# The last four output tiles in another order: tile three behind the first half of tile four, and both halves of tile four in PSUM banks of the gate pool

## The chip, the cores and the metric

The kernel runs on one core of one Trainium2 chip. The metric is device time in microseconds (us) of one execution. The kernel before takes 214.47 us, the median of three runs (214.2 to 214.63).

A core has five engines with an instruction stream each, which wait for one another through counting semaphores: TensorE (PE in the profile; its weight loads are PEld), VectorE (DVE), ScalarE (ACT), GpSimd (POOL) and SyncE (SP), which here mainly issues DMAs. A name with a q (PEq, SPq) is the engine's sequencer: waits, branches and DMA issues.

## The reference, cut to what matters

The inputs are one sequence of 2048 rows of 448 numbers, in bf16. Both branches read the same normalised rows, and their results are added to the input.

```python
def _A_ref(x, wqkv, wo):          # 16 heads of 28, causal window of 256 rows
    q, k, v = heads(x @ wqkv)
    scores = where(0 <= i - j < 256, q @ k.T * 28 ** -0.5, -1e9)
    return (softmax(scores) @ v) @ wo

def _B_ref(x, w_gate, w_up, w_down):   # 448 -> 1792 -> 448
    return (gelu(x @ w_gate) * (x @ w_up)) @ w_down

xn = layernorm(A_x)
out = A_x + _A_ref(xn, A_wqkv, A_wo) + _B_ref(xn, B_w_gate, B_w_up, B_w_down)
```

## The kernel before, in words

The 2048 rows are handled in four query blocks of 512 (`qb` 0 to 3), each of four tiles of 128 rows. A block goes through attention (scores, softmax weights, the product with v, scaling into `oN`), then through the feed-forward part (`gated`: seven pairs of gate and up matmuls, GELU on ScalarE, the product on VectorE into `hT`), and last through `gen_down`, which makes the output rows. The whole order is written out by hand: each engine works its instructions in the order in which the Python code emits them. For blocks 0 to 2 the steps of `gen_down` are spread between the next block's attention steps. For block 3 nothing follows, so `gen_down(3)` stands at the end of the program alone. The change touches only that end.

One output tile is a sum of 18 matmuls into one PSUM bank: 14 with `hT` and `wd` (contraction over 1792), and 4 with `oN` and `wo`. `gen_down` names three lists of them: `main`, ten `hT` chunks that are ready early; `late`, the four chunks of the last two gate pairs; `os`, the four `oN` chunks. `part` issues one such list for a tile, `whole` opens a tile and issues all 18. `begin` takes a bank, and `end` does the rest: VectorE adds the input rows (`res`, L382), the bank is given back, SyncE stores the result (L384). `res` has two buffers that are used in turn, so an addition waits until the store that read its buffer two results ago has landed. The second half of tile four (`lo` above 0) has a buffer of its own, of tag `wa`.

The rows of the last block's tiles are called one to four here (`tt` 0 to 3, rows 1536 to 2047), the column halves of tile four 4a and 4b (224 columns each). Before the change the order is: `main` of one and two; `late` of one and two; `main` and `late` of three; `os` of one, two and three; then all 18 of 4a and all 18 of 4b. In tiles two and three each matmul is issued as two of 224 columns (`ws`, L390), in tile one as one of 448.

PSUM has eight banks. Four (`b0` to `b3`) are handed out by `take` and returned by `give`, with `held` as the list of those in use. The other four are two buffers of two banks each, of tag `s` in the pool `phase[0].pool`; the gates use them in turn (`gt`), ScalarE's GELU reads them, and after the last gate they are free.

The tile framework derives the waits between engines from the tiles that instructions read and write: a matmul that writes to a tile waits, where needed, for the instructions that read the tile before.

Two things lie between the steps. VectorE computes a flag from the softmax sums (L874 to L883), and after 48 steps of `gen_down(3)` every engine loads it (L887); at the very end each engine branches on it around a general path, which does not run here. After the last addition POOL copies the last result twice (L890, L891), and VectorE writes one column (L892).

Of the kernel before, what the change touches and what calls it, by code (L numbers as in the profile page):

```python
# [13 lines left out]
f32 = mybir.dt.float32  # L14
i32 = mybir.dt.int32

S, D, H, Dh, F = 2048, 448, 16, 28, 1792
P = 128
NT = S // P
NF = F // P  # L20
QB, NB = 512, 4
# [6 lines left out]
def kernel(  # L28
# [11 lines left out]
    nc = tc.nc  # L40
# [8 lines left out]
    phase = [None]  # L49
# [152 lines left out]
    held = {}  # L202

    def take(name, cols=QB, tag=None):

        tag = tag or spare[0]
        spare.remove(tag)  # L210
        ps = psum.tile([P, QB], f32, name=name, tag=tag, bufs=1)[:, 0:cols]
        held[id(ps)] = tag, ps
        return ps

    def give(*tiles):
        for ps in tiles:
            spare.append(held.pop(id(ps))[0])
# [94 lines left out]
    def gen_pairs(qb, order):  # L312

        def v_pair(t):
            two = [take("pv", D) for _ in range(2)]
            for c in range(7):
                for hi, ps in enumerate(two):
                    r = slice(64 * hi, 64 * hi + 64)
                    w = wv[r, 3, :] if c == 6 else wv[r, c // 2, :] if c % 2 == hi else wvs[r, c // 2, :]
                    nc.tensor.matmul(ps, lhsT=xchunk(qb, hi, c, (t + hi) * P, P), rhs=w, start=c == 0, stop=c == 6,  # L320
                                     tile_position=(64 * hi, 0), skip_group_check=True)
                if c < 6:
                    yield
            for i in range(2):
                v_copy(t + i, two[i], nc.vector.tensor_copy if i or not t % 4 or qb == 1 else nc.scalar.copy)
            yield

        def qk_pair(g):
            two = [take("p" + part) for part in "qk"]
            for c in range(7):  # L330
                for hi, ps in enumerate(two):
                    r, hs = slice(64 * hi, 64 * hi + 64), slice(4 * g, 4 * g + 4)
                    w = w3p[r, hs, :] if c == 6 else (wqp, wkp)[hi][r, c // 2, hs, :] if c % 2 == hi else wsq[r, c // 2, hs, :]
                    nc.tensor.matmul(ps, lhsT=w.rearrange("p h d -> p (h d)"), rhs=xchunk(qb, hi, c, qb * QB, QB), start=c == 0,  # L334
                                     stop=c == 6, tile_position=(64 * hi, 0), skip_group_check=True)
                if c < 6:
                    yield
            qk_copies(qb, g, *two, nc.vector.tensor_copy if (g != 1) == (qb == 1) else nc.scalar.copy)
            yield

        return chain(*(v_pair(4 * qb + n) if kind == "v" else qk_pair(n) for kind, n in order))
# [25 lines left out]
    def gen_down(qb):  # L367

        hT, oN = hTs[qb], oNs[qb]
        fs = [(hT, wd, f) for f in range(NF)]  # L370
        main, late, os = fs[0:5] + fs[7:12], [fs[f] for f in (5, 12, 6, 13)], [(oN, wo, g) for g in range(4)]

        def begin(tt, lo=0, up=D):
            return tt, take("po", up - lo), lo, up

        def end(tt, po, lo, up):
            t, w = 4 * qb + tt, up - lo
            if lo:
                res = work.tile([P, 2 * QB], bf16, name="res", tag="wa", bufs=1)
            else:  # L380
                res = work.tile([P, D], bf16, name="res", bufs=2)
            nc.vector.tensor_tensor(out=res[:, 0:w], in0=po[:, 0:w], in1=x_sb[:, t, lo:up], op=ALU.add)  # L382
            give(po)
            nc.sync.dma_start(out=outv[:, t, lo:up], in_=res[:, 0:w])  # L384
            last_res[:] = [res]

        def part(o, terms, start=False, stop=False):
            tt, po, lo, up = o
            w = up - lo
            ws = (0, w // 2, w) if 4 * qb + tt in (NT - 3, NT - 2) else (0, w)  # L390
            for n, (x, wt, k) in enumerate(terms):
                for a, b in zip(ws, ws[1:]):
                    nc.tensor.matmul(po[:, a:b], lhsT=x[:, k, tt * P:(tt + 1) * P], rhs=wt[:, k, lo + a:lo + b],  # L393
                                     start=start and n == a == 0, stop=stop and n == len(terms) - 1, skip_group_check=True)
                if stop and n == len(terms) - 1:
                    end(*o)
                yield

        def whole(terms, *o):
            yield from part(begin(*o), terms, True, True)  # L400

        if qb < NB - 1:
            two = [begin(tt) for tt in range(2)]
            for o in two:
                yield from part(o, main + late, True)
            for o in two:
                yield from part(o, os[0:3])
            for tt, po, *_ in two:
                r = slice(64 * tt, 64 * tt + 64)
                nc.tensor.matmul(po, lhsT=oN[r, 3, tt * P:(tt + 1) * P], rhs=wo[r, 3, :], start=False, stop=True,  # L410
                                 tile_position=(64 * tt, 0), skip_group_check=True)
            for o in two:
                end(*o)
            yield
            for tt in (2, 3):
                yield from whole(main + late + os, tt)
        else:
            three = [begin(tt) for tt in range(3)]
            for terms, start in ((main, True), (late, False)):
                for o in three[0:2]:  # L420
                    yield from part(o, terms, start)
            yield from part(three[2], main + late, True)
            for o in three:
                yield from part(o, os, False, True)
            for lo, up in ((0, D // 2), (D // 2, D)):
                yield from whole(main + late + os, 3, lo, up)

    def new_hT(qb):
        hT = blk.tile([P, NF, QB], bf16, name="hT", tag="hT")
# [369 lines left out]
    for qb in range(NB):  # L799
# [4 lines left out]
        if qb == 0:  # L804
# [3 lines left out]
            w = gen_pairs(1, (("v", 0), ("v", 2), ("k", 0), ("k", 1), ("k", 2)))  # L808
# [4 lines left out]
                    [lambda: stat(11), (w, 7), lambda: rstd(8, 4), "sums", "inverse", (w, 7)]]  # L813
        else:
            d = gen_down(qb - 1)
            if qb < 3:
                u = gen_pairs(qb + 1, (("v", 0), ("k", 0), ("v", 2), ("k", 1), ("k", 2)))
# [64 lines left out]
    nc.vector.tensor_reduce(out=ok1, in_=okr, axis=AX.X, op=ALU.min)  # L882
    nc.vector.tensor_copy(out=flag[:, :], in_=ok1)  # L883
    last = gen_down(NB - 1)
    for _ in range(48):
        next(last)
# [136 lines left out]
```

## Time and profile before

| what | value |
|---|---|
| time, median of three runs | 214.47 us (214.2 to 214.63) |
| span of the profiled execution, first to last instruction | 213.1 us |
| PE busy | 207.6 us, 97% of the span |
| DVE, ACT, POOL busy | 74%, 62%, 23% |
| share of PE in the chain that ended last | 94% |
| last block's output matmuls on PE (L393) | 195.24 to 209.2 us |
| last addition on VectorE | 209.21 to 209.60 us |

No separate device time is listed for the profiled execution; the median time stands 1.4 us above its span, which is what lies outside the first and the last instruction.

How to read the profile: times in rows of the timeline are microseconds from the span's start, then the length of the merged row; a matmul's length contains its run through the array, so matmuls that follow each other overlap in the rows, and their spacing is what counts. In brackets stands how long the engine sat idle before a row, and what ended the wait. In the waits view a row reads: who waited, for whom, total time, how often, the longest.

### The profile page before, as it was taken

The numbers are of one execution on the slowest core, as the hardware profiler recorded it, in microseconds if no ns is written. First come the engines' busy times: TensorE is split into PE (matmuls) and PEld (weight loads), VectorE is DVE, ScalarE is ACT, GpSimd is POOL, SyncE is SP. The second block draws the span as 40 slices with busy tenths as digits, with TensorE's granted clock in tenths as the row PEclk, the third lists the DMA queues.
The fourth block names the chain that finished last, engine by engine and source line by source line (L and its number), as shares of the span: only waits on it lengthen the run. The fifth ranks groups of instructions, "written<-read, shape, count | busy, mean of one in ns | idle before, by whom it ended". The sixth has DMA issues, their size and how long they took to land.

```text
span 213.1 us, 6428 instructions
## 1 busy us (share of the span) xinstructions
PE 207.6 (97%) x2722; PEld 101.2 (47%) x2722; DVE 157.5 (74%) x355; ACT 131.6 (62%) x123; POOL 48.6 (23%) x86
## 2 busy tenths in 40 slices
PE   7999999999999999999999999999999999999992
PEld 2433444444454545444445445444445444544992
DVE  7899998999767985796536997495483898479531
ACT  4699578566777977423777887532676877665000
POOL 5287658451000220041000201022000022006001
PEclk9999999999999999999999999999999999999998
DMA  6999969979420101003421000001000101000011
GB/s 184 280 221 215 106 172 220 243 241 171 110 53 25 37 20 26 8 5 65 74 74 46 25 0 29 20 0 30 16 3 0 47 4 45 6 0 0 26 45 49
DMA packets 23993, 15.67 MB, mean 74 GB/s; under 512 B 9208, under 2 KB 23832, under 8 KB 23960
## 3 DMA queue, kind: packets, MB, share of 16 engines
q1 hardware_dynamic: 22918, 14.87, 31.2%
q8 instruction: 22, 0.36, 0.7%
q10 hardware_dynamic: 1042, 0.34, 0.7%
q14 instruction: 11, 0.09, 0.1%
HBM read 9.26 MB, written 2.41 MB: 55 GB/s over the span
## 4 chain that ended last, share of the span: by engine, by line
PE 94%; DVE 1%; ACT 1%; DMA 1%; issue 1%; DVEq 0%; ACTq 0%
PE po L393 26%; PE gt L456 20%; PE u L456 12%; PE ue L456 8%; PE pq L334 7%; PE sc L652 6%; PE ov L624 5%; PE pv L320 4%; PE pq L191 2%; PE pv L191 1%; DMA x_sb<-in_A_x_dram 1%; ACT p_sb L656 1%; DVE st L155 1%; PE s L191 1%; PE pk L191 1%
## 5 line engine op out<-in xcount | busy, mean ns | idle before, releaser
L656 ACT ACTIVATE p_sb<-sc 128x2048 bf16<-128x2048 f32 x39 | 73.2, 1878 | 20.5 <-PE sc L652 13.5
L496 ACT ACTIVATE p_sb<-gt 128x1024 bf16<-128x1024 f32 x28 | 28.7, 1025 | 33.6 <-PE gt L456 30.7
L591 POOL TENSOR_TENSOR oN<-oc,l 128x512 bf16<-128x512 f32 x16 | 21.5, 1355 | 120.0 <-DVE l L604 120.0
L393 PE MATMUL po<-wd,hT 128*128 128x448 bf16 (+1 forms) x266 | 46.2, 324 | 0.0
L456 PE MATMUL gt<-xnT,wg 64*128 64x512 bf16 x224 | 45.6, 376 | 0.0
L456 PE MATMUL gt<-xsw,wg 64*128 64x512 bf16 x168 | 40.7, 376 | 0.0
L504 DVE TENSOR_TENSOR hT<-p_sb,u 128x512 bf16<-128x512 bf16 x34 | 21.9, 677 | 16.0 <-PE u L456 15.8
L572 DVE TENSOR_TENSOR p_sb<-p_sb,masks 128x256 bf16<-128x256 bf16 (+1 forms) x90 | 27.8, 363 | 7.6 <-ACT p_sb L656 7.6
L393 PEld LDWEIGHTS <-hT 128*128 128x128 bf16 x266 | 24.5, 98 | 16.8 <-issue 2.2
L456 PEld LDWEIGHTS <-wg 64*128 64x128 bf16 x392 | 19.0, 94 | 22.5 <-issue 0.2
L456 PEld LDWEIGHTS <-wu 64*128 64x128 bf16 x392 | 18.7, 94 | 22.4 <-issue 0.8
L456 PE MATMUL u<-xnT,wu 64*128 64x512 bf16 x136 | 28.1, 376 | 0.0
L456 PE MATMUL u<-xsw,wu 64*128 64x512 bf16 x102 | 24.7, 376 | 0.0
L382 DVE TENSOR_TENSOR res<-po,x_sb 128x448 bf16<-128x448 f32 (+1 forms) x17 | 9.8, 592 | 11.6 <-PE po L393 9.3
L456 PE MATMUL ue<-xnT,wu 64*128 64x512 bf16 x88 | 18.0, 377 | 0.0
L652 PE MATMUL sc<-qT,kT 28*64 28x320 bf16 (+7 forms) x648 | 16.4, 261 | 0.1
L456 PE MATMUL ue<-xsw,wu 64*128 64x512 bf16 x66 | 16.4, 377 | 0.0
L582 POOL TENSOR_SCALAR_AFFINE_SELECT p_sb<-p_sb 128x512 bf16<-128x512 bf16 (+1 forms) x21 | 14.2, 702 | 6.6 <-ACT p_sb L656 6.5
L609 DVE TENSOR_TENSOR oc<-oc,ov 128x512 f32<-128x512 f32 x12 | 8.2, 681 | 8.7 <-ACT oc L608 8.7
L652 PEld LDWEIGHTS <-kT 28*64 28x64 bf16 (+1 forms) x648 | 7.5, 102 | 13.3 <-issue 12.0
L393 PE MATMUL po<-wo,oN 128*128 128x448 bf16 (+1 forms) x70 | 13.0, 320 | 0.0
L473 DVE CAST hT<-ue 128x512 bf16<-128x512 f32 x18 | 11.6, 679 | 1.9 <-PE ue L456 1.8
(108 smaller groups left out, 276.9 us busy)
## 6 DMA issues: line engine op xcount, KB each, us to landing
out_dram<-res SPq DMA_DIRECT2D x15, 112.0 KB
x_sb<-in_A_x_dram SPq DMA_DIRECT2D x3, 448.0 KB
wd<-in_B_w_down_dram SPq DMA_DIRECT2D x3, 448.0 KB
xsw<-xnT SPq DMA_DIRECT2D x6, 192.0 KB
wu<-in_B_w_up_dram SPq DMA_DIRECT2D x2, 560.0 KB
wg<-in_B_w_gate_dram SPq DMA_DIRECT2D x2, 448.0 KB
wg<-in_B_w_gate_dram SPq DMA_DIRECT2D x2, 336.0 KB
wraw<-in_A_wqkv_dram SPq DMA_DIRECT2D x2, 252.0 KB
```

What stands on the lines that cost most here:

```text
L334: nc.tensor.matmul(ps, lhsT=w.rearrange("p h d -> p (h d)"), rhs=xchunk(qb, hi, c, qb * QB, QB), start=c == 0, stop=c == 6, tile_position= ...
L393: nc.tensor.matmul(po[:, a:b], lhsT=x[:, k, tt * P:(tt + 1) * P], rhs=wt[:, k, lo + a:lo + b], start=start and n == a == 0, stop=stop and ...
L456: nc.tensor.matmul(ps, lhsT=w[64 * hi:64 * hi + 64, c, p * P:(p + 1) * P], rhs=xchunk(qb, hi, c, qb * QB, QB), start=c == 0, stop=c == 6, ...
L473: copy(out=hTs[qb][:, p + 7 * i, :], in_=us[i])
L496: nc.scalar.activation(out=ges[p][:, :, :], in_=gt[:, :, :], func=ACT.Gelu_apprx_tanh)
L504: nc.vector.tensor_tensor(out=hT[:, p + 7 * i, :], in0=ge[:, i, :], in1=u, op=ALU.mult)
L572: nc.vector.tensor_tensor(out=reg, in0=reg, in1=m, op=ALU.mult)
L582: nc.gpsimd.affine_select(out=reg, in_=reg, pattern=mid + [[1 if diag else -1, min(w, P)]], compare_op=ALU.is_ge, fill=0.0, base=0 if diag ...
L591: nc.gpsimd.tensor_tensor(out=oN[:, g, :], in0=oc[:, :], in1=inv, op=ALU.mult)
L624: nc.tensor.matmul(ov[half or 0][32 * j:32 * j + 32, q0:q0 + nq], lhsT=v_sb[r, kt, 4 * g + j, :], rhs=p_sb[r, j, col:col + nq], start=n == ...
L652: nc.tensor.matmul(ss[k0:k0 + nk, j, col:col + nq], lhsT=kT[r, g, kt * P + k0:kt * P + k0 + nk], rhs=qT[r, g, ring(qb).start + q0:ring(qb) ...
L656: nc.scalar.activation(out=p_sb[:, :, 0:ncol], in_=ss[:, :, 0:ncol], func=ACT.Exp, scale=SCALE)
```

## The change

Six things change, all in `gen_down`, and only for block 3 but for the `ws` lines, which in the other blocks did nothing.

- The split of tiles two and three into matmuls of 224 columns goes; they are 448 wide.
- Only tiles one and two take a bank at the start. 4a and 4b get the two banks of a tile `pl`, one buffer of tag `s` of the gate pool.
- 4a takes the place of tile three's `main` and `late`, and then of its `os`.
- Then follow the ten `main` of 4b, all 18 of tile three, and last the eight remaining of 4b (`late` and `os`).
- The additions and stores follow: one, two, 4a, three, 4b, in place of one, two, three, 4a, 4b. The two buffers of `res` are taken by one and 4a, and by two and three.
- `end` gives a bank back only if it is one that `take` handed out.

```diff
-            give(po)
+            if id(po) in held:
+                give(po)
...
-            ws = (0, w // 2, w) if 4 * qb + tt in (NT - 3, NT - 2) else (0, w)
             for n, (x, wt, k) in enumerate(terms):
-                for a, b in zip(ws, ws[1:]):
-                    nc.tensor.matmul(po[:, a:b], lhsT=x[:, k, tt * P:(tt + 1) * P], rhs=wt[:, k, lo + a:lo + b],
-                                     start=start and n == a == 0, stop=stop and n == len(terms) - 1, skip_group_check=True)
+                nc.tensor.matmul(po[:, 0:w], lhsT=x[:, k, tt * P:(tt + 1) * P], rhs=wt[:, k, lo:up],
+                                 start=start and n == 0, stop=stop and n == len(terms) - 1, skip_group_check=True)
...
-            three = [begin(tt) for tt in range(3)]
+            two = [begin(tt) for tt in range(2)]
+            ends = phase[0].pool.tile([P, 2, QB], f32, name="pl", tag="s")
+            first, last = ((3, ends[:, i, 0:D // 2], i * D // 2, (i + 1) * D // 2) for i in range(2))
             for terms, start in ((main, True), (late, False)):
-                for o in three[0:2]:
+                for o in two:
                     yield from part(o, terms, start)
-            yield from part(three[2], main + late, True)
-            for o in three:
+            yield from part(first, main + late, True)
+            for o in (*two, first):
                 yield from part(o, os, False, True)
-            for lo, up in ((0, D // 2), (D // 2, D)):
-                yield from whole(main + late + os, 3, lo, up)
+            yield from part(last, main, True)
+            yield from whole(main + late + os, 2)
+            yield from part(last, late + os, False, True)
```

## The prediction, made before the changed kernel had run

> **What bounds the kernel now.** I read the page's busy shares first, then the chain that ended last, then the timeline of the end, engine by engine, and the waits there.
>
> ```profile
> PE 207.6 (97%) x2722; PEld 101.2 (47%) x2722; DVE 157.5 (74%) x355; ACT 131.6 (62%) x123; POOL 48.6 (23%) x86
> PE 94%; DVE 1%; ACT 1%; DMA 1%; issue 1%; DVEq 0%; ACTq 0%
> 195.31 13.88 PE po L393 x126
> 209.19 0.02 issue
> 209.21 0.39 DVE res L382
> ```
>
> PE is busy 97% of the span and is 94% of the chain. At the end the chain is 13.88 us of output matmuls, then the last addition. So whatever makes PE wait among those 126 matmuls moves the end by as much, and whatever shortens the way from the last matmul to the end counts fully too.
>
> ```profile
> 203.27 2.45 PE L393 MATMUL po<-wo,oN 128*128 128x448 bf16 x20
> 205.56 1.50 PE L393 MATMUL po<-wd,hT 128*128 128x224 bf16 x14
> 206.90 0.55 PE L393 MATMUL po<-wo,oN 128*128 128x224 bf16 x4
> 207.28 1.50 PE L393 MATMUL po<-wd,hT 128*128 128x224 bf16 x14
> 208.63 0.55 PE L393 MATMUL po<-wo,oN 128*128 128x224 bf16 x4
> ```
>
> These are tile endings on PE, without a gap. The spacing of a 224-wide matmul is (206.90 - 205.56) / 14 = 0.096 us. The 20 of 203.27 are 4 of 448 (tile one) and 16 of 224: (205.56 - 203.27 - 16 x 0.0958) / 4 = 0.189 us for a 448-wide one.
>
> ```profile
> 204.23 1.39 DVE L382 TENSOR_TENSOR res<-po,x_sb 128x448 bf16<-128x448 f32 x2 [4.01 <-PE po L393]
> 206.73 0.62 DVE L382 TENSOR_TENSOR res<-po,x_sb 128x448 bf16<-128x448 f32 x1 [1.11 <-DMA out_dram<-res]
> 208.02 0.39 DVE L382 TENSOR_TENSOR res<-po,x_sb 128x224 bf16<-128x224 f32 x1 [0.66 <-DMA out_dram<-res]
> 209.21 0.39 DVE L382 TENSOR_TENSOR res<-po,x_sb 128x224 bf16<-128x224 f32 x1 [0.80 <-PE po L393]
> 204.88 0.36 SPq L384 DMA_DIRECT2D out_dram<-res  x1
> DVE res L382 <- DMA out_dram<-res: 1.8, 2, 1.1
> ```
>
> The third row of additions is the one to see: tile three's sum was complete at 205.56, but its addition began at 206.73, because its `res` buffer is tile one's, whose store was issued at 204.88. Issue to release is 206.73 - 204.88 = 1.85 us. In the kernel before that wait costs nothing: PE was then busy with 4a in another bank.
>
> **The change part by part.** *Wider matmuls.* 36 pairs of 224 (2 x 0.0958 = 0.192) become 36 of 0.189: -0.09 us on PE, all on the path. The row and the spacing decide this; the column count is otherwise the same.
>
> *The order up to the second sum.* PE enters the output matmuls at 195.24 as before. `hT` is ready in the same order, since the first 28 steps are the same. 4a's `main` and `late` are 14 x 0.096 = 1.34 us where tile three's took 28 x 0.096 = 2.68. So `os` of tile one starts at 203.27 - 1.34 - 14 x 0.0024 = 201.9 in place of 203.27. It needs `oN` 1.4 us sooner.
>
> ```profile
> L351 SPq DMA_DIRECT2D o<-oN x3: 335/351/381, 196.4 to 197.2; - x3
> L356 SPq DMA_DIRECT2D oN<-o x4: 250/256/292, 197.9 to 199.0; - x4
> 198.77 0.52 POOL L365 MEMSET oN<- 64x512 bf16 x1 [2.37 <-DMA o<-oN]
> 200.08 0.14 DVE L883 CAST flag<-g 1x1 int32<-1x1 f32 x1
> L887 PEldq TENSOR_LOAD <-flag x1: 487/487/487, 202.3 to 202.3; - x1
> ```
>
> The collecting DMAs were last issued at 197.2 and released POOL at 198.77, 1.56 us later; the last delivering one is issued at 199.0, so it lands at about 200.6, by the store's 1.85 at 200.9. That is 1.0 us ahead of 201.9. POOL's memset ends at 199.3. The flag is ready at 200.2, and PE's load of it (0.49 us) stands, as before, behind the queue of matmuls already handed over. I take nothing for either; if PE's sequencer reached them late, it would cost the few tenths by which its lead falls short.
>
> *The banks from the gates.* `pl` is the buffer of the last gate but one.
>
> ```profile
> 193.89 1.02 ACT L496 ACTIVATE p_sb<-gt 128x1024 bf16<-128x1024 f32 x1 [0.54 <-PE gt L456]
> 195.40 1.02 ACT L496 ACTIVATE p_sb<-gt 128x1024 bf16<-128x1024 f32 x1 [0.49 <-PE gt L456]
> ```
>
> ScalarE has read it by 194.91, and 4a's first matmul comes at about 200.5: no wait. Tile three takes a bank that is long free.
>
> *The new wait, which decides.* 4a and 4b are two banks, but one tile. The built program, read for its waits, has this:
>
> ```
> VectorE's count: 349 flag, 350 addition of one, 351 of two, 352 of 4a
> PE, first matmul of 4b (tile pl): waits for VectorE's count >= 352
> VectorE, addition of 4a: waits for the store of tile one, and for count >= 350
> ```
>
> So 4b's ten `main` matmuls may not start before VectorE has read 4a, though they write to the other bank; and 4a's addition waits for tile one's store. Before, 4b's first matmul waited only for count 350, the addition of one, long past. Everything else on PE (tile three, the rest of 4b) is queued in order behind that matmul, and nothing covers it. The times:
>
> - `os` of one: 201.9 + 3 x 0.189 is the last one's start, 202.45. Before, the start of that matmul was 203.27 + 0.57 = 203.84 and the addition began at 204.23, 0.39 later. So now 202.84, and 0.62 later, 203.46, it ends (the two of 204.23 take 1.39 with a gap).
> - Its store is issued 0.03 after (204.85 to 204.88 before): 203.49. 4a's addition is released 1.85 later: 205.34. It is 224 wide, 0.39 us: ends 205.73.
> - PE is through with 4a's `os` at 201.9 + 8 x 0.189 + 4 x 0.096 = 203.8. 4b starts at about 205.8: **a stall of 2.0 us**.
>
> Bounds: below, if 4a's addition did not have to wait for the store, it would start 0.3 after 4a's last matmul (209.21 against the last matmul at 208.63 + 3 x 0.096 = 208.92), at 204.0, end at 204.4, and the stall would be 0.6; above, a store that is slower by a half gives 2.9. The row of 1.85 is the same buffer, the same shape and the same queue, so I take 2.0.
>
> *After the stall.* 10 x 0.096 + 18 x 0.189 + 8 x 0.096 = 5.1 us of matmuls. Tile three's addition is ready 0.39 after its last matmul starts, lasts 0.62, and is over about 0.14 us before 4b's sum is complete (8 x 0.096 = 0.77 after tile three's last): it just fits, and tile two's store has landed by then (issued near 204.8, plus 1.85). If it missed, the last addition would be late by some tenths.
>
> *The last store.* SP issues tile three's store and 4b's about 0.5 us apart instead of 1.2.
>
> ```profile
> L384 SPq DMA_DIRECT2D out_dram<-res x17: 332/361/847, 62.4 to 209.6; - x17
> 209.63 0.85 SPq L384 DMA_DIRECT2D out_dram<-res  x1
> L897 PEldq COMPARE_BRANCH  x1: 392/392/392, 207.3 to 207.3; - x1
> 208.45:210.10 1.65, 0.72 (x8) 0.47 (x5) 0.39 (x1) 0.00 (x0) 0.36 (x1) 1.00 0.27 69
> 210.10:210.90 0.80, 0.00 (x0) 0.00 (x0) 0.06 (x1) 0.00 (x0) 0.38 (x2) 1.00 0.06 12
> 210.90:211.35 0.45, 0.00 (x0) 0.00 (x0) 0.00 (x0) 0.00 (x0) 0.00 (x0) 0.87 0.47 129
> ```
>
> Of 17 stores the last one alone took 0.85 us to issue, against 0.36, and its data moved only after 210.9 (the last columns: DMA share, GB/s). Before, stores at 207.39, 208.44 and 209.63 followed each other closely, with PE's branch to the end (207.3) among them; after, 4a's store lies over 5 us ahead of the last. So the last issue may fall back to 0.36. Bounds 0 and -0.49; I take -0.4, nearer the 16 rows of 0.33 to 0.38. The two stores close together could give part of it back.
>
> *The sum:* -0.09 + 2.0 - 0.4 = +1.5 us. The profiled span of 213.08 becomes 214.6, and with the 1.4 us outside it, 214.47 becomes **216.0 us** (+0.7%).
>
> **The rivals.** *The stall also halves PE's clock.* This speaks for it:
>
> ```profile
> 207.82:211.23 3.41, 1.35 (x15) 1.10 (x12) 0.84 (x3) 0.00 (x0) 0.74 (x2) 1.00 0.26 71
> 211.23:213.08 1.85, 0.00 (x0) 0.00 (x0) 0.00 (x0) 0.00 (x0) 0.00 (x0) 0.50 0.04 11
> ```
>
> The granted clock went from 1.00 to 0.50 at 211.23, 2.06 us after the last matmul had ended. A pause of 2.0 us, about 1.85 by that count, is nearly as long. If it drops the clock, and for as long as the row of 3.41 us, 1.7 us of work is lost: 217.7 us. Against it: the pause is a little shorter than the one seen, and if the clock is judged in fixed stretches, it would have to lie inside one. *The Trainium skill's page "TensorE: Matmul & The Clock Gate", in the part on the HAM clock gate, says the clock is halved after an idle window of about 3.4 us; by that rule the stall leaves the clock alone and the sum stays. The row above disagrees: the stretch of 3.41 us before the drop held 1.35 us of PE work.*
>
> *The store is not in the way*: 4a's addition runs when its sum is complete, the stall is 0.6, and the end gains 0.5: 214.47 + 0.6 - 0.5 = 214.6, the same. Against it stands the row with 1.11 us of waiting for just this buffer.
>
> *No stall, and faster.* Two banks are two banks: if PE goes on into 4b, 214.47 - 0.5 = 214.0. It decides once 4a is read before 203.8. For it speaks only that the banks are distinct; against it the wait in the program, on a count that cannot be reached before 204.4. *The Trainium skill's page "Perfetto Trace Analysis", under Optimizing Tensor Performance, says that matmul groups which rotate through different banks overlap one group's evacuation with the next one's matmuls; by that rule it would be 214.0. No row here shows two banks of one tile in use that way.*
>
> **How the numbers follow.** The stall without a drop in clock 0.70 (its own range 215.5 to 216.6: last issue at 0.85 gives 216.4, a quicker store 215.6); with a drop 0.19 (217.3 to 217.9); store not in the way 0.06; no stall 0.05. To leave out no more than 0.2 the range takes in the drop: 215.3 to 217.8. The time that a measurement of this kernel tells from no change is 0.2%, 0.43 us. Faster 0.05, same 0.05, slower 0.90.
>
> **What would show it.** On PE, a gap of 1.8 to 2.1 us ahead of ten 224-wide matmuls at about 205.8, ended by the addition of VectorE; on VectorE, a 224-wide addition that waits some 1.3 us for a store and ends just before. PE otherwise without gaps from 195.2, and `os` of tile one at 201.9. The last store's issue at 0.36. PEclk 0.5 within the last 8 us would show the drop. The prediction is wrong if there is no gap before 4b, or if the gap ends without that addition.

## The result, and the profile after

The changed kernel takes 216.6 us (median of six executions, 216.32 to 218.88) against 214.55 us (six, 214.2 to 215.02): a ratio of 1.0123, 95% interval 1.0098 to 1.0148. It is slower, inside the range given, 0.6 us above the time forecast. The six executions fall into two groups: four at 216.32 to 216.68 with a mean granted clock of 0.999 or 1.000, two at 218.23 and 218.88 with 0.992, both above the range. The first group is called the full-clock group here, the second the lowered-clock group. The profiled execution is of the second (218.23 us, span 216.4).

The chain that ended last, after, in order of time (start, length, what):

```profile
195.26 5.40 PE po L392 x28
200.67 1.34 PE pl L392 x14
202.01 0.77 PE po L392 x4
202.78 0.02 issue
202.80 0.64 DVE res L382
203.44 0.02 issue
203.46 2.03 DMA out_dram<-res
...
205.61 0.40 DVE res L382
206.01 0.04 issue
206.05 1.66 PE pl L392 x10
207.71 4.53 PE po L392 x18
212.25 0.78 PE pl L392 x8
```

Before, this stretch was 13.88 us of PE and nothing else. Now it leaves PE at tile one's sum (202.78), goes through VectorE's addition, tile one's store and the addition of 4a, and comes back to PE at 206.05 with 4b's `main`. The same seen from PE, from VectorE and in the waits:

```profile
203.36 0.55 PE L392 MATMUL pl<-wo,oN 128*128 128x224 bf16 x4
206.05 1.66 PE L392 MATMUL pl<-wd,hT 128*128 128x224 bf16 x10 [2.15 <-DVE res L382]
207.51 3.98 PE L392 MATMUL po<-wd,hT 128*128 128x448 bf16 x14
205.61 0.39 DVE L382 TENSOR_TENSOR res<-pl,x_sb 128x224 bf16<-128x224 f32 x1 [1.42 <-DMA out_dram<-res]
PE pl L392 <- DVE res L382: 2.1, 1, 2.1
```

PE stands idle for 2.15 us ahead of 4b. Then ten 224-wide matmuls take 207.51 - 206.05 = 1.46 us where 0.96 was due, and the 448-wide ones come 0.37 us apart at first. The stages say why (the column before the DMA share is the granted clock):

```profile
203.05:206.46 3.41, 1.26 (x12) 0.92 (x11) 1.40 (x3) 0.00 (x0) 0.00 (x0) 1.00 0.24 75
206.46:209.87 3.41, 3.41 (x15) 1.86 (x13) 0.00 (x0) 0.00 (x0) 0.00 (x0) 0.50 0.06 17
209.87:213.28 3.41, 3.15 (x21) 1.78 (x19) 0.85 (x2) 0.00 (x0) 0.00 (x0) 1.00 0.02 5
```

For 3.41 us after the pause PE ran at half its clock. At full clock that stretch would have held 1.71 us more work; that is most of the 2.1 us between the medians of the two groups (216.5 and 218.6).

### The profile page after: what moved, and what is told of

The parts are those of the page before. It is cut to its first block, busy times and chain, and to the rows that moved or that the text cites. A ratio compares the mean times of both kernels' runs of the same rounds, so it can differ in the third digit from the quotient of the medians.

```text
span 216.4 us, 6352 instructions
## 1 busy us (share of the span) xinstructions
PE 208.6 (96%) x2682; PEld 98.0 (45%) x2686; DVE 157.5 (73%) x355; ACT 131.6 (61%) x123; POOL 48.7 (22%) x86
## 4 chain that ended last, share of the span: by engine, by line
PE 93%; DMA 2%; DVE 2%; ACT 1%; issue 1%; DVEq 0%; ACTq 0%
PE po L392 24%; PE gt L458 20%; PE u L458 12%; PE ue L458 8%; PE pq L334 6%; PE sc L654 6%; PE ov L626 5%; PE pv L320 4%; PE pl L392 2%; PE pq L191 2%; PE pv L191 1%; DMA x_sb<-in_A_x_dram 1%; DMA out_dram<-res 1%; ACT p_sb L658 1%; DVE st L155 1%
## 5 line engine op out<-in xcount | busy, mean ns | idle before, releaser
L392 PE MATMUL po<-wd,hT 128*128 128x448 bf16 x210 | 44.5, 360 | 0.0
L392 PEld LDWEIGHTS <-hT 128*128 128x128 bf16 x238 | 22.6, 100 | 22.7 <-issue 5.9
L382 DVE TENSOR_TENSOR res<-po,x_sb 128x448 bf16<-128x448 f32 x15 | 9.0, 619 | 13.9 <-PE po L392 13.4
L392 PE MATMUL po<-wo,oN 128*128 128x448 bf16 x54 | 12.0, 352 | 0.0
```

The costliest lines, as they stand in the source:

```text
L392: nc.tensor.matmul(po[:, 0:w], lhsT=x[:, k, tt * P:(tt + 1) * P], rhs=wt[:, k, lo:up], start=start and n == 0, stop=stop and n == len(term ...
```

## The experiments

Theory 1, from the prediction: the loss is the wait of 4b on 4a's addition, made by the shared tile, lengthened by tile one's store, and in some executions doubled by the clock. Its rivals: the new order itself costs (the early need of `oN`, the close stores, the last two additions), or the lowered clock has a cause other than the idleness.

**The changed kernel again, for the share of the two groups and a second profile.** No edit.

> The changed kernel once more, unchanged, for the share of executions with a lowered clock, and for a second profile. If the clock is judged in fixed stretches of 3.41 us whose phase against the program is free, and some 2.1 us of idleness in one is enough, then a gap of 2.1 to 2.3 us falls into one stretch in about a third of the executions: about 3 of 10 at 218 to 219 us with a mean clock of 0.992, the others at 216.3 to 216.7 with 1.0 or 0.999. The gap on PE is 2.0 to 2.3 us, depending on how fast the first store lands.

Measured: 216.24, 218.57, 218.12 and 216.49 us, mean clocks 1.000, 0.992, 0.992, 0.999. With the first six, four of ten are in the lowered-clock group (218.12 to 218.88), and the median of the other six is 216.5. The profile is of the full-clock group (216.24 us, span 214.5):

```profile
201.94 1.68 PE L392 MATMUL po<-wo,oN 128*128 128x448 bf16 x8
205.85 1.12 PE L392 MATMUL pl<-wd,hT 128*128 128x224 bf16 x10 [1.85 <-DVE res L382]
203.55 0.36 SPq L385 DMA_DIRECT2D out_dram<-res  x1
205.41 0.39 DVE L382 TENSOR_TENSOR res<-pl,x_sb 128x224 bf16<-128x224 f32 x1 [1.13 <-DMA out_dram<-res]
202.58:206.00 3.42, 1.57 (x12) 0.95 (x11) 1.64 (x3) 0.00 (x0) 0.00 (x0) 1.00 0.20 66
206.00:209.41 3.41, 3.41 (x24) 2.18 (x23) 0.00 (x0) 0.00 (x0) 0.00 (x0) 1.00 0.09 25
```

4b starts at 205.85, and the clock stays at 1.00. Tile one's store released the addition 205.41 - 203.55 = 1.86 us after its issue here, and 205.61 - 203.46 = 2.15 in the first profile; the gap differs by that, 0.3 us. With the 1.7 us of the lowered clock this makes 2.0 us, about the distance between the groups.

**Two tiles for the two halves: the cause itself.**

```diff
-            ends = phase[0].pool.tile([P, 2, QB], f32, name="pl", tag="s")
-            first, last = ((3, ends[:, i, 0:D // 2], ...
+            ends = [phase[0].pool.tile([P, 2, QB], f32, name="pl", tag="s") for _ in range(2)]
+            first, last = ((3, ends[i][:, 0, 0:D // 2], ...
```

> The changed kernel, with the two banks of 4a and 4b taken as two tiles of the gate pool instead of two halves of one; order and widths as changed. Theory 1 (the wait on the addition of 4a comes from the shared tile and is the whole loss): no gap on PE before 4b, whose ten matmuls start at about 203.75 us, last matmul 2.3 us earlier than in the changed kernel, no execution with a lowered clock, and 214.1 to 214.4 us, 0.0 to 0.2% below the kernel before. Theory 2 (the new order itself costs, by the early need of oN, the close stores or the last two additions): PE still waits or the end is late, 215 us or more.

Measured: 214.29 us (twelve executions, 214.01 to 214.48), ratio 0.9983 (0.9963 to 1.0002); lowest mean clock 0.997, as in the kernel before.

```profile
203.43 0.55 PE L392 MATMUL pl<-wo,oN 128*128 128x224 bf16 x4
203.81 1.12 PE L392 MATMUL pl<-wd,hT 128*128 128x224 bf16 x10
205.38 0.39 DVE L382 TENSOR_TENSOR res<-pl,x_sb 128x224 bf16<-128x224 f32 x1 [1.13 <-DMA out_dram<-res]
208.37 0.62 DVE L382 TENSOR_TENSOR res<-po,x_sb 128x448 bf16<-128x448 f32 x1 [2.60 <-PE po L392]
209.14 0.39 DVE L382 TENSOR_TENSOR res<-pl,x_sb 128x224 bf16<-128x224 f32 x1
```

The addition of 4a still waits 1.13 us for the store, but PE goes from 4a into 4b without a gap (203.81). The whole loss goes with the shared tile, so the order and the widths cost nothing. The last two additions just fit, as forecast: 208.99 and 209.14.

**4a's result in a buffer of its own: the store's part.**

```diff
-            if lo:
+            if w < D:
                 res = work.tile([P, 2 * QB], bf16, name="res", tag="wa", bufs=1)
```

> The changed kernel, with the result of 4a in the buffer of tag wa, which 4b's uses later, so that its addition needs no landed store; 4a and 4b still share one tile. Theory 1: the wait on PE stays, but ends when the addition of 4a ends: addition from about 204.0 to 204.4, 4b from about 204.45 instead of 206.05, a gap of 0.7 us in place of 2.3, no lowered clock, and 216.5 - 1.6 = 214.9 us. If the store is not what holds the addition, the time stays at 216.5 us.

Measured: 214.95 us (ten executions, 214.69 to 215.64), ratio 1.0016 (0.9995 to 1.0037).

```profile
204.55 1.12 PE L392 MATMUL pl<-wd,hT 128*128 128x224 bf16 x10 [0.63 <-DVE res L382]
204.12 0.38 DVE L382 TENSOR_TENSOR res<-pl,x_sb 128x224 bf16<-128x224 f32 x1
```

The wait stays and is 0.63 us long; the rest of the gap was the store. Of the 2.2 us between the changed kernel's full-clock group (216.5) and the two tiles (214.3), the store's part is 1.5 and the addition's 0.7.

**The gap filled with matmuls nobody reads: is the lowered clock idleness?**

```diff
+            fill = take("fill", D)
+            for n in range(11):
+                nc.tensor.matmul(fill, lhsT=hT[:, n, 0:P], rhs=wd[:, n, :], start=True, stop=True)
+            give(fill)
             yield from part(last, main, True)
```

> The changed kernel with eleven matmuls of 448 columns, whose result nobody reads, put into a spare bank between 4a's last matmul and 4b's first: 11 x 0.189 = 2.08 us of PE work inside the gap of 2.3 us. Theory 1: the gap is idle time that costs by its length alone, and the lowered clock comes from the idleness: the time of the undisturbed executions stays at 216.4 to 216.7 us, PE waits only about 0.2 us ahead of 4b, and no execution shows 218 us or a mean clock of 0.992. If the lowered clock has another cause, some executions still show 218 us. If the filler costs, the time is above 216.7 in all.

Measured: 216.3 us (six executions, 216.0 to 216.66), mean clocks 0.998 to 1.000. 2.08 us of useless work cost nothing against the full-clock group, and no execution fell into the other one. Six executions say this weakly: at four in ten, six without a drop would still come about one time in twenty. The row shows the filler in the gap:

```profile
203.75 2.24 PE L428 MATMUL fill<-wd,hT 128*128 128x448 bf16 x11
205.83 1.12 PE L392 MATMUL pl<-wd,hT 128*128 128x224 bf16 x10
```

**A longer gap.** One buffer for the results of one, two and 4a.

```diff
-            if lo:
+            if qb == NB - 1 and (tt < 2 or w < D and not lo):
                 res = work.tile([P, 2 * QB], bf16, name="res", tag="wa", bufs=1)
```

> The changed kernel with one result buffer for tiles one, two and 4a, so that the additions of two and of 4a each wait for the store before: the gap on PE ahead of 4b grows from 2.3 to about 4.9 us (two stores of 2.0 to 2.1 us each with their additions of 0.62 and 0.39). The gap alone: 216.5 + 2.6 = 219.1 us. Theory K (the clock is judged in fixed stretches of 3.41 us, and one with about 2.1 us or more of idle PE lowers it for the next): a gap of 4.9 us always has such a stretch, so every execution shows a mean clock below 0.998 and pays 0.3 to 1.7 us more, 219.4 to 220.8 us. Theory L (a stretch must be idle as a whole): some executions keep the full clock, at 219.1 us.

Measured: 220.31, 222.34, 221.31 and 221.5 us, mean clocks 0.992, 0.985, 0.984, 0.984. All four lost clock, as theory K has it; three of them lie above its 220.8. A shortfall of 0.016 is twice that of one stretch, so the three probably had two lowered stretches; no trace shows them. The profiled one had one:

```profile
208.12 1.12 PE L392 MATMUL pl<-wd,hT 128*128 128x224 bf16 x10 [4.36 <-DVE res L382]
202.29:205.71 3.42, 1.47 (x10) 0.85 (x9) 1.15 (x2) 0.00 (x0) 0.00 (x0) 1.00 0.13 41
205.71:209.12 3.41, 1.00 (x11) 1.00 (x11) 0.49 (x2) 0.00 (x0) 0.00 (x0) 1.00 0.15 47
209.12:212.53 3.41, 3.41 (x12) 1.42 (x10) 0.00 (x0) 0.00 (x0) 0.00 (x0) 0.50 0.02 4
```

The gap of 4.36 us is cut in two by the edge at 205.71. The stretch before it held 1.47 us of PE work and had no effect; the one after held 1.00 and halved the clock of the next. The gap is 4.36 us and not 4.9, because the two stores took 1.87 and 1.84 us. Two lowered stretches would need some 2 us of idle PE in each, nearly the whole of such a gap, so why three of four executions seem to have had two stays open.

**The kernel before again: what lies outside the span, and the last store.** No edit.

> The kernel before, unchanged, for a second profile of it. In the changed kernel's runs the time stood 1.7 to 1.8 us above the span (216.32 over a span of 214.6), and the prediction took 1.4 us. Theory A: what lies outside the span is the same 1.7 us for both kernels, and the profiled execution of before was about 0.3 us slower than the median of 214.5, because its last store took 0.85 us to issue. Then this profile shows a span near 212.8 us, a last store issued in 0.33 to 0.37 us, and the gain of 0.4 us that the prediction took for it is no gain against the median. Theory B: the late issue is the rule in this kernel: again 0.85 us, span about 213.1, and 1.4 us outside.

Measured: 214.67 us (ten executions, 214.13 to 215.03), ratio 0.9998 (0.9978 to 1.0018). Half of each theory holds. Time less span is 1.66 to 1.86 us in every one of 81 executions of this kernel, median 1.74, and their median span is 212.9: a profiled span of 213.1 belongs to a time of about 214.8, not 214.47. But the late issue came again:

```profile
209.67 0.79 SPq L384 DMA_DIRECT2D out_dram<-res  x1
```

**The wider matmuls alone**, in the old order:

```diff
-            ws = (0, w // 2, w) if 4 * qb + tt in (NT - 3, NT - 2) else (0, w)
+            ws = (0, w)
```

> The kernel before with one part of the change alone: tiles two and three as matmuls of 448 columns, in the old order and the old banks. By the spacing (2 x 0.0958 against 0.189 us, 36 times) PE's last matmul comes 0.09 us sooner, and nothing else moves: a time 0.1 us (0.04%) below the kernel before, 214.4 to 214.5, and a span about 0.1 us below its span. The last eighteen matmuls are of 224 columns as before, so PE's branch still stands 2.3 us ahead of the last store's issue, and that issue should again take about 0.8 us in the profile.

Measured: 214.6 us (twelve executions), ratio 1.0005 (0.9993 to 1.0016). 0.09 us is below what the times can tell. PE's rows do show it:

```profile
195.18 8.12 PE L393 MATMUL po<-wd,hT 128*128 128x448 bf16 x42
208.47 0.55 PE L393 MATMUL po<-wo,oN 128*128 128x224 bf16 x4
```

From the first output matmul to the first of the last four are 13.29 us here, against 208.63 - 195.24 = 13.39 before. With two tiles, in the new order, it is 208.56 - 195.26 = 13.30. The last store's issue took 0.62 us.

**Two tiles, tile three's matmuls halved again: the branch and the last store.** `ws` is back for tile three only (`4 * qb + tt == NT - 2`).

> The kernel with two tiles for 4a and 4b (214.29 us, last store issued in 0.33 us), with tile three's matmuls halved again as in the kernel before; the order stays. PE's queue is about 17 matmuls deep, and now the last 44 are of 224 columns, so PE's branch should move from 3.3 to about 2.3 us ahead of the last store. Theory T (the last store's late issue comes from the fetch of instructions after PE's branch, which then collides with the last stores): the issue takes about 0.8 us again, and the time rises by 0.05 for the matmuls and 0.2 to 0.5 for the issue, to 214.5 to 214.8. Theory U (the late issue comes from three stores within 2.3 us before it, which this order does not have): the issue stays at 0.33 us, and the time at 214.3 to 214.4.

Measured: 214.29 us (eleven executions, 214.14 to 215.36), ratio 0.9999 (0.9987 to 1.0011).

```profile
209.41 0.33 SPq L385 DMA_DIRECT2D out_dram<-res  x1
L901 PEldq COMPARE_BRANCH  x1: 397/397/397, 207.1 to 207.1; - x1
```

The branch moved to 2.3 us ahead of the last store, as meant, and the issue stayed at 0.33. So theory T in this form falls: the place of the branch alone does not make the issue late. That order also lacks the stores shortly before, as theory U has it. The traced packets say that the fetch has a part all the same: in the three profiles with a late last issue (before, its repetition, the wider matmuls alone) a packet of 16 KB of instructions ended at 210.10, 210.09 and 209.73 us, and the issue ended 0.37 us after it each time; here that packet was over before the last two stores moved data.

The same pairing stands in the traces far from the end. The second of two stores at 62.9 us took 0.75 us to issue in the changed kernel and 0.55 us with two tiles, and ended 0.40 and 0.38 us after a packet of 16 KB (63.22 and 63.11 us); with 4a's buffer of its own the packet was over at 62.79 us, before that issue began, and it took 0.36 us. So three stores in a row, as in theory U, are not needed: the late issue goes with a packet still moving when a second store is issued. Not every issue is held so: three for another tile (`kT`) that began or ended during such a packet at 69 us took 0.37 to 0.41 us in the changed kernel. No run moved the packet by itself, so the cause stays open.

Tile one's store, which sets the gap, goes with such a packet too. Where a packet of 16 KB ended 0.11 to 0.20 us after that store's issue began (the changed kernel again, two tiles, the filled gap, the longer gap) the store took 1.85 to 1.87 us from issue to release; where it ended 0.31 us or more after (two tiles again, this run, the changed kernel) it took 2.02, 1.99 and 2.15 us. That is a pairing in seven traces, and not an experiment either.

**The two tiles once more.** No edit to that kernel.

> The kernel with two tiles for 4a and 4b once more, unchanged, because its first ratio to the kernel before (0.9983, 0.9963 to 1.0002) leaves open whether it is faster. By the spans (212.3 to 212.7 in twelve executions, against 212.3 to 214.3 before) the order is worth 0.1 to 0.3 us, the matmuls' 0.09 and the last store's issue where that was late: 214.2 to 214.4 us, a ratio of 0.9983 to 0.9993. If the first ratio was scatter, it is 0.9995 to 1.0005.

Measured: 214.4 us (twelve executions, 214.08 to 215.12) against 214.71 (17): ratio 0.9990 (0.9979 to 1.0000). Twice the same side, each time with the edge of the interval at no change, and the run with tile three halved, 0.05 us more of matmuls, had 0.9999. The order without its wait is worth at most 0.1 to 0.2%, some 0.2 to 0.4 us, and is hardly to be told from nothing.

## Why the prediction was right

*The bound and the chain.* Right: whatever makes PE wait in its last matmuls moves the end by as much; the chain after shows each link that was named.

*The wider matmuls, -0.09 us.* Right on PE, where the stretch of output matmuls fell from 13.39 to 13.29 us; too small to be told in the times.

*The order up to the second sum.* Right: `os` of tile one begins at 201.85 in the first profile and 201.94 in the second, without a wait for `oN`; forecast 201.9.

*The new wait.* Right in place and cause, shown by taking it away. Forecast: 4b at 205.8, a stall of 2.0 us. The second profile has 205.85; the first 206.05, because the store took 2.15 instead of 1.85. The forecast counts the stall from the moment at which the next matmul could have started; so counted it is 2.0 us in the second profile and 2.3 in the first, where the profile, which counts from the end of the last record, has 1.85 and 2.15. Without the store the gap is 0.63 us by the profile and 0.8 by the forecast's count, where the lower bound said 0.6.

*After the stall.* Right: the last additions fit, by 0.14 us.

*The last store, -0.4 us.* 0.33 us in both profiles of the changed kernel, so against the profiled execution of before the term holds: its span of 213.08 was to become 214.6, and the full-clock executions have 214.5 to 215.0. The reason given for it, the stores close together with PE's branch among them, was not shown; what the traces pair with a late issue is the packet of instructions. Against the median execution the term is smaller: with two tiles, where the matmuls and the last store should save 0.49 us together, the times fell by 0.2 to 0.4.

*The step that was mis-sized* is the last of the sum, "with the 1.4 us outside it". The profiled execution of before was taken for a median one; it was 0.3 us longer, and what lies outside the span is 1.74 us. 214.6 + 1.74 = 216.3, against 216.24 to 216.68 measured in the full-clock group, whose median is 216.5; the first store's scatter, 0.3 us between the two profiles, is large enough for the rest.

*The rivals.* The drop in clock was given 0.19 and 217.3 to 217.9; it came in four of ten executions, at 218.1 to 218.9, all above that and above the range of 215.3 to 217.8. Its price was right (1.7 us); it was counted from 216.0, and the one traced execution that had it also had the longer pause. That the median of the first six stayed in the range is partly luck: with four of the six lowered it would have been above 218. The drop was thought less likely because the pause was shorter than the one seen before; the limit lies just there, and a store slower by 0.3 us takes the pause across it. *By the Trainium skill's page "TensorE: Matmul & The Clock Gate", in the part on the HAM clock gate, an idle window of about 3.4 us is what lowers the clock; the stretch with 1.26 us of PE work in 3.41 contradicts it.* The rival without a stall, 214.0, came about once each half had a tile of its own, at 214.29 and 214.40. *The Trainium skill's page "Perfetto Trace Analysis", under Optimizing Tensor Performance, says that groups in different banks overlap with the evacuation; by the row at 203.81 us the trace agrees with two tiles, and by the row at 206.05 not with two banks of one tile.*

## What to carry to other kernels

Two banks are independent only if whatever sets the waits knows them as two: look in the built program for the count on which the first matmul of a group waits, and follow who raises it. An addition that waits for its result buffer costs nothing until somebody waits for the addition. And before a span is turned into a time, check what lies between the two over several executions.

## What the runs showed of the hardware that I had not expected

The granted clock is judged in fixed stretches of 3.41 us: all changes seen are whole numbers of such stretches apart (206.46 and 209.87 us in the changed kernel, 209.12 and 212.53 with the longer gap; before, from the rise at 6.43 us to the drop at 211.23, 60 of them). Half clock followed a stretch with 1.35 us of PE work (before, at its end), with 1.39 (before again, at its end), with 1.26 (after) and with 1.00 (the longer gap); full clock followed 1.47 (the longer gap) and 1.57 (after, again).

```profile
207.83:211.24 3.41, 1.39 (x15) 1.13 (x12) 0.84 (x3) 0.00 (x0) 0.74 (x2) 1.00 0.25 72
211.24:213.06 1.82, 0.00 (x0) 0.00 (x0) 0.00 (x0) 0.00 (x0) 0.00 (x0) 0.50 0.03 10
```

So the limit here lies between 1.39 and 1.47 us of 3.41, some 41 to 43% busy, and a pause of 2.0 us is enough when it falls into one stretch. In each of these stretches PE's idle time was one pause, so the runs do not tell a limit on the busy share from one on the pause.
